# Heads grouped by parity: eight 64x32 TensorE tiles in place of block-diagonal pairs, in a landmark-attention and MLP kernel

## The chip, the cores and the metric

The kernel runs on one core of a Trainium2 chip. The metric is device time in microseconds of one execution. A kernel is timed in several executions; one execution is also recorded by the hardware profiler, and the rows below come from that one.

## The reference, cut to what matters

Eight batches of landmark attention (8 heads, 576 positions, head size 64, 32 landmarks) feed two MLPs. All operands are fp32.

```python
q_lm = q.reshape(B, H, 32, 18, D).mean(axis=3)      # k_lm in the same way
A, Bm, C = sm(q, k_lm), sm(q_lm, k_lm), sm(q_lm, k) # sm: scaled softmax scores
Z = Bm.T / (norm1(Bm) * norminf(Bm) + 1e-6)
for _ in range(6):
    Z = 2 * Z - Z @ Bm @ Z
attn = A @ Z @ C @ v
h = x @ w_in;  g = where(h > 0, h, exp(min(h, 0)) - 1);  x = g @ w_out   # 512 -> 2048 -> 512
y = max(x @ w1, x @ w2, x @ w3) @ w_out2                                  # 512 -> 768 -> 512
```

## The kernel before, in words

q and k arrive transposed, so that 128 partitions hold two heads (64 rows each); `load_qk` brings four heads at a time (`g` is 0 or 1). The attention output is never formed: A, the softmax of q against the landmarks, is multiplied by W' = (Z C v) w_in, which `w_step` makes for each batch out of `m_step`'s 64 values per head and landmark. Phase 1 runs over eight batches `b`, each in 32 slots: a slot is one `h_mm` (six matmuls of A's high and low parts with W', line 597) and one `x_mm` (twelve matmuls with w_out, line 628), so 18 mainline matmuls of 288 columns a slot, 576 a batch. Behind `h_mm` come two ACT operations (relu and exp), a DVE operation, an ACT cast and a POOL or DVE subtraction; `x_mm` follows three slots later (`LAG`). Phase 2 (lines 903 and 1012, the second MLP) follows; the change does not touch it.

The attention of batch b+1 is spread over the slots of batch b: `plan` names the slot behind which each step is emitted (`att_steps` for b of 2 and more, `SECOND_SLOTS` for b of 1). For batch 0 it stands ahead of everything, in the order of the string `ORDER` (B, A and V are three streams of steps, c a step of the weights' conversion). DVE's order there is the program's (`manual_schedule`); elsewhere a list scheduler orders each engine's queue by dependencies and priority, and each engine works its queue in order.

A score matmul takes K = 128: for two heads at once, `sums` has POOL spread the landmark sums into a block-diagonal copy (`qbd`, `kbd`), so that a 128x64 weight tile holds both heads. Two such matmuls, `p2` of 0 and 1, write the lower and the upper 64 partitions of one PSUM bank. Each fp32 matmul stands in the trace as two matmuls and two weight loads. `score_c` (C and Bm, line 278) makes two such pairs for each `g`, one for each half of 288 positions; `score_a` (line 327) does the same for A; `w_step` (line 564) makes one pair of 512 columns for each of four column blocks `n` and each `g`, with the copy `mbd` that `m_step` makes out of a masked copy `v2`. `cv` (line 395) multiplies C with v in five chunks, each a pair of 128 columns of which half is masked away afterwards.

PSUM's eight banks: four for `x_mm` (`ps_x`), two for `h_mm` (`ps_h`), two for the attention and W' (`ps_a`, one bank a tile, two tiles). In batch 0 ahead of the mainline, `att_ps` also hands out the banks of `ps_x`. W' is read out of PSUM by an ACT cast (line 572, the high part) and a DVE subtraction (line 576, the low part).

Of the kernel before, what the change touches and what calls it, by code (L numbers as in the profile page):

```python
# [19 lines left out]
def landmark_attention_mlp_maxout_kernel(  # L20
# [18 lines left out]
    P = 128  # L39
# [24 lines left out]
    SECOND_SLOTS = [4, 5, 6, 6, 7, 7, 8, 11, 11, 11, 12, 12, 12, 13, 13, 13]  # L64
    SECOND_SLOTS += [13, 14, 15, 16, 18, 19, 20, 20, 21, 23, 24, 26, 26, 26, 26]

    ORDER = "BBBBBABVVBAVVBVcBABcVABcABcABccBcBABcAcB"
# [26 lines left out]
    ps_a = tc.alloc_tile_pool(name="ps_a", bufs=2, space=PSUM)  # L94
# [43 lines left out]
    class Conversions:  # L138
# [54 lines left out]

    hm = const.tile([P, 4], F32, name="hm")
    dm = const.tile([P, 2], F32, name="dm")
    pm = const.tile([P, 2], F32, name="pm")
# [7 lines left out]
        out=dm, in_=ident.rearrange("p (h j) -> p h j", h=2), op=ALU.add, axis=AX.X  # L204
    )
    nc.vector.tensor_reduce(
        out=eye, in_=ident.rearrange("p (h j) -> p j h", h=4), op=ALU.add, axis=AX.X
    )
    nc.vector.tensor_tensor(out=pm, in0=hm[:, 0:2], in1=hm[:, 2:4], op=ALU.add)
# [10 lines left out]
    def att_ps(b, name):  # L220

        if b == 0 and spare[0] >= 0:
            spare[0] += 1
            n = spare[0] % 6
            if n < 4:
                return ps_x.tile([P, 512], F32, tag=f"x{n}", name=name)
        return ps_a.tile([P, 512], F32, tag="a", name=name)

    def load_qk(b, g, nm):
        n = S + M if nm == "k" else S  # L230
        t = att.tile([P, 2, n], F32, tag=nm + "T", name=nm + "T", bufs=2)
        src = (k if nm == "k" else q)[b, g * 2 * P : (g + 1) * 2 * P, :]
        nc.sync.dma_start(out=t[:, :, :S], in_=src.rearrange("(r p) s -> p r s", p=P))
        state[nm, b, g] = t
# [10 lines left out]
    def sums(b, g, nm):  # L245
        t = state[nm, b, g]
        if nm == "k":
            so = t[:, :, S : S + M]
        else:
            so = att.tile([P, 2, M], F32, tag="qs", name="qs")  # L250
# [7 lines left out]
        sh = [P, 2, 2, M]  # L258
        nc.gpsimd.tensor_tensor(
            out=bd,  # L260
            in0=so.unsqueeze(2).to_broadcast(sh),
            in1=dm.unsqueeze(1).unsqueeze(3).to_broadcast(sh),
            op=ALU.mult,
        )
        state[nm + "bd", b, g] = bd

    def score_c(b, g):
        kT, qbd = state["k", b, g], state["qbd", b, g]
        if g == 0:
            state["bb", b] = att.tile([P, 4, M], F32, tag="bb", name="bb")  # L270
        e = att.tile([P, S], F32, tag="s", name="e", bufs=2)
        mx = att.tile([P, 2], F32, tag="mx", name="mx")
        pcs = []
        for half in range(2):
            n = HF + (M if half else 0)
            pc = att_ps(b, "pc")
            for p2 in range(2):
                nc.tensor.matmul(  # L278
                    pc[64 * p2 : 64 * p2 + 64, :n],
                    qbd[:, p2].rearrange("p a m -> p (a m)"),  # L280
                    kT[:, p2, half * HF : half * HF + n],
                    start=True,
                    stop=True,
                )
            nc.vector.tensor_reduce(
                out=mx[:, half : half + 1], in_=pc[:, :HF], op=ALU.max, axis=AX.X
            )
            pcs.append(pc)
        nb = att.tile([P, 1], F32, tag="nb", name="nb")
        nc.vector.tensor_scalar(  # L290
            out=nb, in0=mx[:, 0:1], scalar1=mx[:, 1:2], scalar2=-s1, op0=ALU.max, op1=ALU.mult
        )
        nc.vector.tensor_copy(state["bb", b][:, g], pcs[1][:, HF : HF + M])
        sm = att.tile([P, 2], F32, tag="sm", name="sm", bufs=2)
        for half in range(2):
            nc.scalar.activation(
                e[:, half * HF : (half + 1) * HF],
                pcs[half][:, :HF],
                AF.Exp,
                bias=nb,  # L300
                scale=s1,
                accum_out=sm[:, half : half + 1],
            )
        state["e", b, g], state["sm", b, g] = e, sm

    def score_c2(b, g):
        sm = state.pop(("sm", b, g))
        rs = att.tile([P, 3], F32, tag="rs", name="rs", bufs=2)
        nc.vector.tensor_scalar(
            out=rs[:, 2:3],  # L310
            in0=sm[:, 0:1],
            scalar1=sm[:, 1:2],
            scalar2=1e-9,
            op0=ALU.add,
            op1=ALU.add,
        )
        nc.vector.reciprocal(rs[:, 2:3], rs[:, 2:3])
        nc.vector.tensor_scalar_mul(rs[:, 0:2], pm, rs[:, 2:3])
        state["rs", b, g] = rs

    def score_a(b, g):
        qT, kbd = state["q", b, g], state["kbd", b, g]
        x = att.tile([P, 2 * NB2, M], F32, tag="s", name="x", bufs=2)
        for half in range(2):
            pa = att_ps(b, "pa")
            for p2 in range(2):
                nc.tensor.matmul(  # L327
                    pa[64 * p2 : 64 * p2 + 64, :HF],
                    kbd[:, p2].rearrange("p a m -> p (a m)"),
                    qT[:, p2, half * HF : (half + 1) * HF],  # L330
                    start=True,
                    stop=True,
                )
            nc.vector.transpose(
                out=x[:, half * NB2 : (half + 1) * NB2].rearrange("p a m -> p (a m)"),
                in_=pa[:, :HF],
            )
        state["x", b, g] = x
# [19 lines left out]
    def soft_a3(b, g):  # L358
# [6 lines left out]
        af = att.tile([P, S], F32, tag="s", name="af", bufs=2)  # L365
# [11 lines left out]
    def exp_t(b, g):  # L377
        e = state.pop(("e", b, g))
        et = att.tile([P, CH, P], F32, tag="et", name="et")
        pt = att_ps(b, "pe")  # L380
# [3 lines left out]
        p2 = att_ps(b, "pe")  # L384
# [4 lines left out]
    def cv(b, g):  # L389
        et, vn, rs = state.pop(("et", b, g)), state["v", b], state["rs", b, g]  # L390
        pt = att_ps(b, "ptv")
        for c in range(CH):
            n = P if c < CH - 1 else TAIL
            for p2 in range(2):
# [7 lines left out]
        vv = rrs[0][:, g, M : M + D]  # L402
        nc.vector.tensor_scalar_mul(vv, pt[:, :D], rs[:, 0:1])
        nc.vector.scalar_tensor_tensor(
            out=vv, in0=pt[:, D:P], scalar=rs[:, 1:2], in1=vv, op0=ALU.mult, op1=ALU.add
        )
# [77 lines left out]
    def bbt(b):  # L484
        bb, td, rc = state["bb", b], state.pop(("td", b)), state["rc", b]
        for gs in groups(b):
            pt = att_ps(b, "pbb")
# [20 lines left out]
    def newton(b, i):  # L508
        cur, nxt, rd = rrs[i % 2], rrs[(i + 1) % 2], state.pop(("rd", b))
        pvs = []  # L510
        for gs in groups(b):
            pt = att_ps(b, "pn")
# [21 lines left out]
        if i == 5:  # L534
            v2 = att.tile([P, 2, 2, D], F32, tag="rd", name="v2", bufs=2)
            nc.gpsimd.tensor_tensor(
                out=v2,
# [827 lines left out]
```

## Time and profile before

| | |
|---|---|
| median of 3 runs | 1436.78 us (1432.18 to 1437.85) |
| the profiled execution | 1435.57 us, of which 1433.8 us are the span from its first to its last instruction |
| busy share of the span | PE 96%, PEld (weight loads) 88%, DVE 64%, POOL 50%, ACT 48% |
| mean granted TensorE clock | 0.977 of full speed |
| chain that ended last | PE 77%, DVE 10%, DMA 6%, issue 3% |

PE is the matmul engine, PEld its weight loads (they overlap the matmuls), DVE VectorE, ACT ScalarE, POOL GpSimd. A matmul's recorded duration contains its way through the array; the rate is read from starts.

### The profile page before, as it was taken

What the parts mean: (1) busy time and instruction counts of PE and PEld (TensorE: products, weight loads), DVE (VectorE), ACT (ScalarE), POOL (GpSimd) and SP (SyncE); (2) the same over time, 40 slices, a digit from 0 to 9 for tenths busy, and PEclk for the clock granted to TensorE, in tenths of its full rate; (3) what the DMA queues carried; (4) which work ended last, traced back from release to release, by engine and by line L of the source; (5) the groups of instructions that cost most, each with busy time, mean ns of one, the idle gap of its engine ahead of it and who ended that gap; (6) DMA issues with size and microseconds to landing.
All of it is one profiled execution on the core that took longest, in us unless ns stands there. A gap on an engine that the chain in (4) does not pass through costs nothing.

```text
span 1433.8 us, 26970 instructions
## 1 busy us (share of the span) xinstructions
PE 1375.8 (96%) x10312; PEld 1256.5 (88%) x10312; DVE 924.4 (64%) x1687; ACT 683.1 (48%) x1554; POOL 717.7 (50%) x717
## 2 busy tenths in 40 slices
PE   5689999999999999999999899899999999998998
PEld 3378788799798797897897899899999999998998
DVE  7998655556456456556454746867776677687773
ACT  4666555555555555555555574322222223335552
POOL 3776324334334344243243565756666666674543
PEclk6789999999999999999999999999999999999999
DMA  9523214024123122141121212212221222238982
GB/s 360 198 85 125 83 63 143 21 71 146 34 74 115 34 97 92 34 138 50 41 83 45 76 33 82 100 68 84 106 82 53 107 82 88 94 129 288 301 261 80
DMA packets 91586, 152.22 MB, mean 106 GB/s; under 512 B 5312, under 2 KB 49472, under 8 KB 91456
## 3 DMA queue, kind: packets, MB, share of 16 engines
q1 hardware_dynamic: 91456, 150.49, 30.7%
q8 instruction: 81, 1.33, 0.4%
q14 instruction: 49, 0.40, 0.1%
HBM read 99.35 MB, written 51.12 MB: 105 GB/s over the span
## 4 chain that ended last, share of the span: by engine, by line
PE 77%; DVE 10%; DMA 6%; issue 3%; ACT 2%; POOL 2%; SPq 0%; DVEq 0%; ACTq 0%; POOLq 0%
PE p L903 24%; PE x L628 23%; PE ph L597 12%; PE p L1012 9%; PE pw L564 4%; DMA words<-in_moe_w_dram 3%; DVE wf L127 2%; PE ptv L395 1%; DMA words<-in_moe_w_out_dram 1%; PE pa L327 1%; DVE wf L123 1%; PE pc L278 1%; PE pn L515 1%; ACT wf L115 1%; DMA hf<-hs 1%
## 5 line engine op out<-in xcount | busy, mean ns | idle before, releaser
L628 PE MATMUL x<-gt,wo 128*128 128x288 f32 x3072 | 480.0, 302 | 6.3 <-DVE wo L100 2.9
L628 PEld LDWEIGHTS x<-gt,wo 128*128 128x128 f32 x3072 | 426.8, 189 | 64.7 <-issue 28.0
L903 PE MATMUL p<-xo,w 128*128 128x256 f32 x3402 | 412.6, 284 | 4.3 <-ACT xo L745 1.7
L903 PEld LDWEIGHTS p<-xo,w 128*128 128x128 f32 x3402 | 410.2, 191 | 6.7 <-ACT xo L745 3.3
L100 POOL TENSOR_TENSOR gt<-eh,gt 128x288 fp32r<-128x288 f32 x243 | 206.8, 853 | 342.3 <-ACT gt L98 337.6
L597 PE MATMUL ph<-ah,wp 128*128 128x288 f32 x1024 | 252.5, 300 | 11.7 <-DVE eh L607 9.7
L607 DVE SCALAR_TENSOR_TENSOR eh<-eh,ph 128x288 f32<-128x288 f32 x256 | 114.3, 447 | 159.3 <-ACT eh L602 151.7
L784 POOL TENSOR_TENSOR u<-s,v 128x512 f32<-128x512 f32 x99 | 137.2, 1386 | 138.6 <-DVE v L782 138.6
L597 PEld LDWEIGHTS ph<-ah,wp 128*128 128x128 f32 x1024 | 180.2, 190 | 28.8 <-DVE eh L607 13.1
L601 ACT ACTIVATE eh<-ph 128x288 f32<-128x288 f32 x256 | 104.7, 410 | 173.3 <-PE ph L597 157.2
L98 ACT CAST gt<-eh 128x288 fp32r<-128x288 f32 x256 | 110.0, 430 | 88.3 <-DVE eh L607 85.9
L597 PE MATMUL ph<-al,wp 128*128 128x288 f32 x512 | 151.9, 297 | 0.0
L773 ACT COPY s<-p 128x512 f32<-128x512 f32 x99 | 57.9, 585 | 185.0 <-PE p L903 155.3
L1012 PE MATMUL p<-wo,ho 128*128 128x256 f32 x1134 | 136.8, 283 | 5.4 <-ACT ho L1000 4.0
L1012 PEld LDWEIGHTS p<-wo,ho 128*128 128x128 f32 x1134 | 136.1, 192 | 6.0 <-ACT ho L1000 4.4
L602 ACT ACTIVATE eh<-eh 128x288 f32<-128x288 f32 x256 | 113.7, 445 | 5.5
L797 DVE TENSOR_TENSOR t<-p,u 128x512 f32<-128x512 f32 x81 | 55.7, 687 | 65.6 <-POOL u L784 62.7
L597 PEld LDWEIGHTS ph<-al,wp 128*128 128x128 f32 x512 | 97.0, 190 | 0.0
L1002 DVE TENSOR_TENSOR ho<-hf,ho 128x768 fp32r<-128x768 f32 x54 | 66.1, 1248 | 17.7 <-ACT ho L1000 16.9
L910 DVE TENSOR_TENSOR t<-t 128x1024 f32<-128x1024 f32 x54 | 71.5, 1325 | 8.7 <-POOL t L787 3.2
L135 POOL TENSOR_TENSOR wf<-wf,words 128x512 uint32<-128x512 uint32 x40 | 55.1, 1379 | 39.5 <-ACT wf L115 18.5
L564 PE MATMUL pw<-w_in_sb,mbd 128*64 128x512 f32 x256 | 72.0, 645 | 0.5 <-ACT mbd L556 0.5
(143 smaller groups left out, 1593.8 us busy)
## 6 DMA issues: line engine op xcount, KB each, us to landing
hf<-hs SPq DMA_DIRECT2D x63, 384.0 KB, 5.0
hs<-t SPq DMA_DIRECT2D x27, 512.0 KB, 3.2
xs<-xo SPq DMA_DIRECT2D x36, 288.0 KB, 2.6
hs<-s SPq DMA_DIRECT2D x27, 384.0 KB, 3.5
qT<-in_q_dram SPq DMA_DIRECT2D x16, 576.0 KB, 3.8
kT<-in_k_dram SPq DMA_DIRECT2D x16, 576.0 KB, 4.8
words<-in_moe_w_dram SPq DMA_DIRECT2D x9, 1024.0 KB, 5.3
xf<-xs SPq DMA_DIRECT2D x9, 1024.0 KB, 5.0
```

Of the source, the lines that this page charges most:

```text
L98: nc.scalar.copy(hi, src)
L100: eng.tensor_tensor(out=lo, in0=src, in1=hi.bitcast(F32), op=ALU.subtract)
L564: nc.tensor.matmul(pt[64 * p2 : 64 * p2 + 64, :], mbd[:, kk], w_in_sb[:, kk, n * 512 : (n + 1) * 512], start=True, stop=True,)
L597: nc.tensor.matmul(ph[:, :HF], a, c, start=(g == 0 and j == 0), stop=(g == 1 and j == 2))
L601: nc.scalar.activation(e, ph[:, :HF], AF.Relu, scale=-1.0)
L602: nc.scalar.activation(e, e, AF.Exp, scale=-1.0)
L607: nc.vector.scalar_tensor_tensor(out=e, in0=e, scalar=1.0, in1=ph[:, :HF], op0=ALU.subtract, op1=ALU.max)
L628: nc.tensor.matmul(xacc[ec][:, :HF], a, gt[:, c], start=(first and j == 0), stop=(last and j == 2),)
L784: nc.gpsimd.tensor_tensor(out=u57, in0=s57, in1=v.unsqueeze(1).to_broadcast([P, 2, 256]), op=ALU.add)
L903: nc.tensor.matmul(dst, l, r, start=(c == 0 and j == 0), stop=(c == 1 and j == 2))
L910: nc.vector.tensor_tensor(out=t, in0=t, in1=cur, op=ALU.max)
L1012: nc.tensor.matmul(dst, l, r, start=(c == 0 and n == 0), stop=(c == NP - 1 and n == 2))
```

## The change

Heads are grouped by parity: group `g` is now the heads on partitions 64g to 64g+63 of the four two-head tiles `j`. A new function `heads` issues eight matmuls in a row, each with K = 64 and 32 weight columns: tile (g, j) reads partitions 64g.. and writes partitions 32j.. of bank g. So both groups' scores of one half, or both groups' W' of one block `n`, come from one call, on the sums themselves: `qbd`, `kbd`, `mbd`, `v2` and the masks `dm` and `pm` go. `ps_a` becomes one tile of two banks (`bufs=1`), handed out as a pair to every step, also to one that uses a single bank. For b of 1 and more, `score_c` copies the scores out of PSUM with ACT and takes the exp from SBUF. `cv` uses four column tiles of 32 with 64 columns in place of two of 64 with 128. The steps' slots and `ORDER` are written anew.

```diff
-    ORDER = "BBBBBABVVBAVVBVcBABcVABcABcABccBcBABcAcB"
+    ORDER = "BBBBBVVABVVBAVcBABcVABcABcABccBcBABccB"
-    ps_a = tc.alloc_tile_pool(name="ps_a", bufs=2, space=PSUM)
+    ps_a = tc.alloc_tile_pool(name="ps_a", bufs=1, space=PSUM)
...
+            n = spare[0] % 3
+            if n < 2:
+                return [
+                    ps_x.tile([P, 512], F32, tag=f"x{2 * n + g}", name=name) for g in range(2)
+                ]
+        t = ps_a.tile([P, 2, 512], F32, tag="a", name=name)
+        return [t[:, g] for g in range(2)]
...
-        bd = att.tile([P, 2, 2, M], F32, tag=nm + "bd", name=nm + "bd")
...
+    def heads(outs, left, right):
+        with tc.manual_schedule(engines={mybir.EngineType.PE}), tc.high_priority(offset=400):
+            for j in (3, 2, 1, 0):
+                for g in range(2):
+                    nc.tensor.matmul(
+                        outs[g][32 * j : 32 * j + 32],
+                        left(j)[64 * g : 64 * g + 64],
+                        right(j)[64 * g : 64 * g + 64],
+                        start=True,
+                        stop=True,
+                    )
+
+    def score_c(b):
+        direct = b == 0
+        es = [att.tile([P, S], F32, tag="s", name="e", bufs=3) for _ in range(2)]
...
+            pcs = att_ps(b, "pc")
+            heads(
+                [pc[:, :n] for pc in pcs],
+                lambda j: state["qs", b, j // 2][:, j % 2],
+                lambda j: state["k", b, j // 2][:, j % 2, half * HF : half * HF + n],
+            )
+            for g in range(2):
+                nc.vector.tensor_reduce(
+                    out=mx[:, g, half : half + 1], in_=pcs[g][:, :HF], op=ALU.max, axis=AX.X
                 )
...
+                if not direct:
+                    nc.scalar.copy(es[g][:, half * HF : (half + 1) * HF], pcs[g][:, :HF])
...
+    def score_a(b):
+            pas = att_ps(b, "pa")
+            heads(
+                [pa[:, :HF] for pa in pas],
+                lambda j: state["ks", b, j // 2][:, j % 2],
+                lambda j: state["q", b, j // 2][:, j % 2, half * HF : (half + 1) * HF],
+            )
+            for g in range(2):
+                nc.vector.transpose(
...
-            for p2 in range(2):
+            for j in range(4):
                 nc.tensor.matmul(
-                    pt[64 * p2 : 64 * p2 + 64, :P],
-                    et[:n, c, 64 * p2 : 64 * p2 + 64],
-                    vn[:n, c, (2 * g + p2) * P : (2 * g + p2 + 1) * P],
+                    pt[32 * j : 32 * j + 32, :D],
+                    et[:n, c, 32 * j : 32 * j + 32],
+                    vn[:n, c, (2 * j + g) * D : (2 * j + g + 1) * D],
...
+    def w_step(b, n, later=False):
+        mt = state["mt", b]
+        pts = att_ps(b, "pw")
+        heads(
+            pts, lambda j: mt[:, j], lambda j: w_in_sb[:, j, n * 512 : (n + 1) * 512]
+        )
...
+    STEP_SLOTS = dict(
+        q0=0, k0=1, q1=2, k1=3, c=5, c20=6, c21=6, e0=6, cv0=7, e1=8, b=8, b2=9, cv1=10, nb=10,
+        bbt=11, n0=12, n1=13, n2=14, n3=15, n4=16, n5=17, a=18, m=19, a10=19, a20=20, a30=20,
+        a11=21, a21=22, a31=23,
+    )
...
+            at(t0 + NSL + 2 * n - 6, w_step, b, n)
```

## Rows read from the trace of the kernel before

**Rows 1.** Windows: length, busy us (count) of PE, PEld, DVE, ACT, POOL; PEclk; DMA
```profile
0.00:53.00 53.00, 29.72 (x124) 16.55 (x125) 43.91 (x110) 24.79 (x57) 24.18 (x27) 0.65 0.91 328
53.00:141.00 88.00, 74.25 (x484) 61.36 (x484) 81.06 (x147) 62.20 (x145) 61.53 (x51) 0.92 0.36 115
141.00:185.00 44.00, 44.00 (x290) 34.49 (x290) 28.24 (x54) 23.70 (x58) 16.20 (x22) 1.00 0.21 70
386.40:487.30 100.90, 100.46 (x724) 87.28 (x723) 55.62 (x128) 55.96 (x139) 37.67 (x46) 1.00 0.24 79
789.00:1433.00 644.00, 626.33 (x5100) 622.15 (x5098) 443.39 (x628) 237.62 (x466) 390.31 (x345) 0.99 0.34 118
```

**Rows 2.** Timeline of PE, two W' pairs: start, us, operation, count
```profile
464.07 0.29 PE L597 MATMUL ph<-ah,wp 128*128 128x288 f32 x1
...
464.86 0.83 PE L628 MATMUL x<-gt,wo 128*128 128x288 f32 x5
465.62 1.08 PE L564 MATMUL pw<-w_in_sb,mbd 128*64 128x512 f32 x4
466.63 0.93 PE L628 MATMUL x<-gt,wo 128*128 128x288 f32 x5
...
468.27 1.08 PE L564 MATMUL pw<-w_in_sb,mbd 128*64 128x512 f32 x4
```

**Rows 3.** Timeline of PE around two pairs of score_a
```profile
247.01 0.71 PE L327 MATMUL pa<-qT,kbd 128*64 128x288 f32 x4
247.65 1.20 PE L628 MATMUL x<-gt,wo 128*128 128x288 f32 x7
248.78 0.71 PE L327 MATMUL pa<-qT,kbd 128*64 128x288 f32 x4
```

**Rows 4.** Timeline of PE around one group's score_c (two pairs)
```profile
387.05 1.25 PE L278 MATMUL pc<-kT,qbd 128*64 128x288 f32 x8
388.22 2.25 PE L628 MATMUL x<-gt,wo 128*128 128x288 f32 x15
390.31 0.29 PE L597 MATMUL ph<-ah,wp 128*128 128x288 f32 x1
```

**Rows 5.** Timeline of PE around one group's cv
```profile
409.25 1.46 PE L395 MATMUL ptv<-v,et 128*64 128x128 f32 x20
410.64 1.85 PE L628 MATMUL x<-gt,wo 128*128 128x288 f32 x12
412.33 0.29 PE L597 MATMUL ph<-ah,wp 128*128 128x288 f32 x1
```

**Rows 6.** Line 564 alone, windows: PE and PEld busy (count), PEclk, DMA
```profile
465.60:465.64 0.04, 0.02 (x2) 0.02 (x2) 1.00 0.00 0
...
466.09:466.12 0.03, 0.03 (x4) 0.00 (x0) 1.00 0.00 0
```

**Rows 7.** Groups by line, 386.4 to 487.3: how W' leaves PSUM
```profile
L576 DVE TENSOR_TENSOR wp<-pw,wp 128x512 fp32r<-128x512 f32 x8 | 5.5, 682 | 1.0 <-ACT wp L572 0.3
...
L572 ACT CAST wp<-pw 128x512 fp32r<-128x512 f32 x8 | 4.7, 587 | 0.8 <-PE pw L564 0.2
```

**Rows 8.** What PE waited for from 185 to 789: total, times, longest
```profile
PE pn L515 <- DVE rr L528: 1.9, 5, 0.4
```

**Rows 9.** Timeline: the last pair of a batch's score_a on PE, and DVE's transposes of it
```profile
450.37 0.71 PE L327 MATMUL pa<-qT,kbd 128*64 128x288 f32 x4
...
457.52 0.83 DVE L334 STREAM_TRANSPOSE x<-pa 128x288 f32<-128x288 f32 x2
```

**Rows 10.** Timeline of the stretch ahead of the mainline: first scores, last sum, v2, first W'
```profile
6.74 2.36 PE L278 MATMUL pc<-kT,qbd 128*64 128x288 f32 x8 [6.74 <-POOL qbd L259]
...
9.59 1.35 DVE L251 TENSOR_REDUCE kT<-kT 128x64 f32<-128x1152 f32 x1
...
45.46 0.99 POOL L536 TENSOR_TENSOR v<-rr,pm 128x256 f32<-128x256 f32 x1 [2.61 <-DVE rr L528]
...
48.20 3.68 PE L564 MATMUL pw<-w_in_sb,mbd 128*64 128x512 f32 x8 [0.46 <-ACT mbd L556]
```

More of the change, by code (lines that the diff above doesn't have):

```diff
@@ L256, in sums @@
         )
-        bd = att.tile([P, 2, 2, M], F32, tag=nm + "bd", name=nm + "bd")
[L258 to L273, printed above, removed]
+        state[nm + "s", b, r] = so
@@ new lines, in score_c @@
+        nc.vector.tensor_reduce(out=nb, in_=mx, op=ALU.max, axis=AX.X)
+        nc.vector.tensor_scalar_mul(nb, nb, -s1)
+        for g in range(2):
+            e = es[g]
+            sm = att.tile([P, 2], F32, tag="sm", name="sm", bufs=2)
+            if direct:
+                for half in range(2):
+                    nc.scalar.activation(
+                        e[:, half * HF : (half + 1) * HF],
+                        kept[half][g][:, :HF],
+                        AF.Exp,
+                        bias=nb[:, g : g + 1],
+                        scale=s1,
+                        accum_out=sm[:, half : half + 1],
+                    )
+            else:
+                nc.scalar.activation(
+                    e, e, AF.Exp, bias=nb[:, g : g + 1], scale=s1, accum_out=sm[:, 0:1]
+                )
+            state["e", b, g], state["sm", b, g] = e, sm
@@ L319, in score_c2 @@
+        if b == 0:
+            nc.vector.tensor_scalar(
+                out=rs,
+                in0=sm[:, 0:1],
+                scalar1=sm[:, 1:2],
+                scalar2=1e-9,
+                op0=ALU.add,
+                op1=ALU.add,
+            )
+        else:
+            nc.vector.tensor_scalar_add(rs, sm[:, 0:1], 1e-9)
+        nc.vector.reciprocal(rs, rs)
         state["rs", b, g] = rs
-    def score_a(b, g):
-        qT, kbd = state["q", b, g], state["kbd", b, g]
-        x = att.tile([P, 2 * NB2, M], F32, tag="s", name="x", bufs=2)
+    def score_a(b):
+        xs_ = [
+            att.tile([P, 2 * NB2, M], F32, tag="s", name="x", bufs=3) for _ in range(2)
+        ]
@@ L340, in soft_a1 @@
+        for g in range(2):
+            state["x", b, g] = xs_[g]
     def soft_a1(b, g):
@@ L1054, in att_steps @@
-            (9, lambda: soft_b2(b)),
-            (10, lambda: cv(b, 1)),
-            (10, lambda: norm_b(b)),
-            (11, lambda: bbt(b)),
+            ("q0", lambda: sums(b, 0, "q")),
+            ("k0", lambda: sums(b, 0, "k")),
+            ("q1", lambda: sums(b, 1, "q")),
+            ("k1", lambda: sums(b, 1, "k")),
+            ("c", lambda: score_c(b)),
+            ("c20", lambda: score_c2(b, 0)),
+            ("c21", lambda: score_c2(b, 1)),
+            ("e0", lambda: exp_t(b, 0)),
@@ L1143, in w_both @@
         conv.upto(index["in", n * KD + KD - 1] + 1)
-        return [w_step(0, n, g, True) for g in range(2)]
+        return w_step(0, n, True)
     def w_end(n):
@@ L1184, in landmark_attention_mlp_maxout_kernel @@
     conv.upto(KD)
[L1185 to L1186 removed]
+    for fn in w_step(0, 0, True):
         gate = fn()
```

229 lines of the change are left out of this document (76 added, 153 removed).

## Prediction

> **What bounds the kernel now.** I read the windows by stage first [rows 1]. In a middle batch of phase 1, 100.9 us long, PE is busy for 100.46 us, at a granted clock of 1.00 (the 2.4 GHz level), while DVE, ACT and POOL are busy for 56, 56 and 38. The table of PE's waits [rows 8] names 1.9 us in five waits, its longest entry, from 185 to 789 us. So what PE issues is the length of a batch there, and a microsecond that it is spared is a microsecond of the kernel. From 141 to 185 PE is busy for the whole 44.00 us as well. From 53 to 141 it is not the bound: DVE is busy for 81 of 88 us, PE for 74. Ahead of 53 us the clock is 0.65 on average and PE idles for nearly half the time: there the end is set by a chain through DVE. Phase 2, 789 to the end, is as full of PE work, none of which the change touches.
>
> Then I priced PE's pieces in the timeline, by starts. A mainline matmul takes one step of 0.132 us: six `h_mm` steps lead from 464.07 to 464.86 [rows 2]. Between the starts of two W' pairs lie 2.65 us and eleven such steps (1.45), so that a W' pair with its way in and out costs 1.20 us. Two pairs of `score_a` lie 1.77 us apart with seven steps (0.92) between them [rows 3]: 0.85 each. For `score_c` [rows 4] 15 steps follow, 3.26 - 1.98 = 1.28; the way in, which this difference does not hold, is 0.10 in rows 2 (464.86 and five steps give 465.52, the pair starts at 465.62). So 1.38 for one group, two pairs back to back. `cv` in the same way [rows 5]: 3.08 - 1.58 + 0.10 = 1.60.
>
> What the reader is to see next is that tiles already run side by side. In [rows 6] both `p2` tiles of a W' pair have their first matmul under way within the first 40 ns; the second two join within 30 ns at 466.09, so that the pair is two waves of two, 0.48 us apart, and not four matmuls in a row.
>
> **The change part by part.** *Scores and W'.* Today a batch spends 2 x 1.38 = 2.76 us on C, 4 x 0.85 = 3.40 on A and 8 x 1.20 = 9.60 on W': 15.76 us. Afterwards it is two, two and four calls of eight tiles. If eight tiles share the two waves as two do now, a call costs today's pair and the starts of six more tiles, for which I take 0.01 us each (two start within the 40 ns window): 0.85 + 0.05 = 0.90 for scores, 1.20 + 0.05 = 1.25 for W'. That is 1.8 + 1.8 + 5.0 = 8.6, a gain of 7.2 us a batch. Whether tiles in the upper and the lower 64 partitions run together is what no row shows; that they don't is a rival below. The other bound, tiles that are no cheaper in fours than in twos, is that rival's upper end. The Trainium skill, TensorE: Matmul & The Clock Gate, Part 3 ("Measured speedup vs the span model"), has row and column tiles running together, 16 of them, with about 4 ns a tile; by it a call would cost 0.03 us less than I take, and the sum would be 1390 us. No run so far shows it for this shape.
>
> This gain counts in full for the attention of batches 2 to 7, which runs beside six PE-bound batches: 6 x 7.2 = 43.2 us. Of batch 1, `score_a` (1.6) and W' (4.6) fall into the PE-bound stretch from 141 to 185: 6.2 us. Its `score_c` and batch 0's W' fall between 53 and 141, where DVE sets the time: nothing, at most 0.96 for the scores and 3 x 1.15 for the blocks, 4.4 us, if PE counted there. Sum: 49.4 us.
>
> *cv.* Ten pairs in waves become ten fours with half the columns. A call's 1.60 us less the way in and out (0.10 each) is 0.14 a wave, an estimate. If a wave shrinks with its columns, half of that goes: 0.7 a call, 1.4 a batch. If a wave is bound by its number of instructions, which doubles, a call gets 1.4 dearer, a batch 2.8. The nearest row is its own, ten waves in either case; I take 0, with -8 and +17 us over six batches as ends.
>
> *The one place in PSUM.* Every step now takes both banks and waits until the step before has left them. For the newton steps, `bbt`, `cv` behind `exp_t`, and `m_step` this adds nothing, since each already needs the result that the evacuation makes. W' calls come every second slot, some six us apart; the release takes the call, one cast and two subtractions in turn, 1.25 + 0.59 + 2 x 0.68 = 3.2 us [rows 7], so PE finds the place free. New waits are three a batch: the second half of `score_c` and of `score_a` behind the first half's evacuation, `exp_t` of group 1 behind `cv` of group 0. Behind such a waiting matmul stand mainline `h_mm` and `x_mm` in PE's queue, and ACT's relu waits for those. The scheduler can put mainline work between the halves, as it does now between dependent newton steps; where it is a little wrong PE waits like the newton steps do [rows 8], up to 0.4 each. I take 0.25 a place, 0.75 a batch, 5 us over seven batches; ends 0 and 1.5 us a place (two transposes of 0.42 [rows 9] and the matmuls' own way out).
>
> The Trainium skill, TensorEngine Tiling (Array Packing), "PSUM Bottleneck", speaks against the change: tiling quickens TensorE and leaves the emptying of PSUM as slow as it was. By it a W' call would cost its two subtractions, 1.36 us, not 1.25, and the sum would be about 1395 us. The row speaks against that here: DVE is free for 45 of 100.9 us [rows 1].
>
> *Other engines.* POOL loses the four masks and `v2` of a batch, DVE two small operations a group; neither sets a batch's time. ACT gets four copies of 288 columns and has two long exps for four short ones: at most 4 x 0.59 (the row of a 512-column cast [rows 7]) on 56 us, covered by 45 idle. If that cover were gone, it would delay relu and so `x_mm` three slots later. No DMA is added or passed; SP's queue sees its transfers sooner, at a DMA share of 0.24.
>
> *Ahead of the mainline* [rows 10]. C's scores start at 6.74 today with one group; now they need all four sums, so not before 10.94, and their exps come some 2 us later, with DVE waiting. On the other side the masked copy `v2` (0.99) leaves the chain into `m_step`, and W' of block 0, 3.68 us at the low clock, halves. I take 0, with 3 us either way.
>
> *Sum.* 49.4 - 5.3 = 44 us off. The profiled execution took 1435.57 us (its span is 1433.8, and 1.8 lie around it); the median is 1436.78, 1.2 above. 1435.6 - 44 gives **1392 us**. With the ends of the small terms (cv, places, start, the stretch from 53 to 141) not all taken together, the forecast's own range is 1377 to 1406.
>
> **The rivals.**
>
> *Row tiles take turns.* The two groups' tiles share columns of the array, and every wave becomes two. A score call then costs up to 0.85 + 2 x 0.29 = 1.4 us (the wave of 288 columns estimated at 0.29 from 0.48 for 512), a W' call 1.20 + 0.96 = 2.2. A batch: 2.8 + 2.8 + 8.8 = 14.4 for 15.76 today, 1.4 us gained; with six batches, 1 us of batch 1 and the 5 us of waits it ends at 1431. If the second load of weights hides, some 0.05 a wave comes back and it is 1425. For it: no row of before has two row tiles. Against: the column tiles run freely.
>
> *The place stalls PE in part.* The three new waits cost their end of 1.5 us each: 4.5 x 7 = 31 us, and 49 - 31 leaves 1418. For it: PE's queue is in order, and two slots of slack are no help within one step. Against: newton steps wait little.
>
> *Slower: `score_a` holds the place.* DVE took the last transposes of a batch 6.5 us after their matmuls had left (451.0 to 457.5 [rows 9]), because its queue had other work first. Today the two banks just stay full. With one place, the second half's call and then `m_step` stand behind such a release in PE's queue. If PE has no other work queued ahead of them, each costs up to 6.5 us; the gain of 7 us a batch is gone at 7 us of such waits a batch, and both together, 13 us in seven batches, give 1435.6 - 49 + 91 = 1478. Against: the scheduler knows of the release and moves these calls behind mainline work.
>
> **How the numbers follow.** Chances: the forecast 0.67, row tiles in turns 0.13, place in part 0.13, slower 0.07. Differences under 0.5% (7 us) can hardly be told from none here. Faster by more: the forecast, the second rival and half of the first, 0.86; the same: the other half of the first, 0.07; slower 0.07. The range of 1375 to 1425 holds the forecast with its own range, the second rival and part of the first, about 8 in 10.
>
> **What would show it.** In the profile after: a middle batch of about 94 us in place of 100.9, with PE still busy throughout; the calls of eight with all eight first matmuls starting within 0.1 us, score calls at 0.90 us and W' calls at 1.25 by the same differences of starts; PE's waits for DVE or ACT under a microsecond a batch. Two starts a wave within a call, or the second group's 0.3 us or more behind the first's, would speak for row tiles in turns. Waits of PE ahead of the second halves, named with the reductions of `mx`, the copies of `e` or the transposes of `x`, would speak for the place. The prediction is wrong if a batch shortens by less than 4 us, if DVE or ACT becomes what PE waits for in the mainline, or if the first W' call, which starts at 48.20 us now [rows 10], moves by more than 3 us.

## The result, and the profile after

The changed kernel took 1450.51 us, the median of four runs, beside 1436.37 for the kernel before in the same comparison: a ratio of 1.010, 95% interval 1.0068 to 1.0132. It is 1% slower. I had predicted 1392 us, 3% faster, and 0.07 for slower.

The profiled execution took 1451.51 us with a span of 1449.5. The windows of the kernel after (length, busy us and count of PE, PEld, DVE, ACT, POOL; PEclk; DMA share, GB/s) answer to [rows 1]: the stretch ahead of the first expert step (the first `h_mm`), batch 0, one middle batch from its first `h_mm` to the next batch's, and that batch cut in two.

```profile
0.00:63.40 63.40, 22.12 (x202) 11.94 (x202) 41.61 (x104) 28.05 (x63) 23.95 (x25) 0.72 0.79 286
63.43:190.10 126.67, 104.04 (x834) 88.56 (x834) 101.84 (x183) 77.85 (x180) 66.92 (x58) 0.90 0.30 98
285.80:389.20 103.40, 97.46 (x843) 85.77 (x843) 54.26 (x124) 56.30 (x140) 35.19 (x41) 0.95 0.22 77
...
285.80:296.00 10.20, 7.27 (x52) 3.40 (x60) 7.34 (x15) 4.71 (x11) 3.13 (x4) 0.58 0.17 59
296.00:389.20 93.20, 90.19 (x799) 82.36 (x795) 46.92 (x110) 51.59 (x130) 32.05 (x37) 0.99 0.23 79
```

The first `h_mm` begins at 63.4 us instead of 52.7. Batch 0 takes 126.7 us instead of 120.4. Batches 1 to 6 together take 602.5 instead of 606.8, and what follows 656.8 instead of 653.8 (2.8 of these 3.0 in batch 7, up to its last `x_mm`). So the loss of 15.7 us in the span is 10.7 at the start, 6.3 in batch 0 and 3.0 at the end, and the steady batches, where I had put nearly the whole gain, return 4.3.

Inside the middle batch the ten microseconds at its front are the odd ones: PE is busy for 7.27 of 10.20 us and the granted clock averages 0.58, close to the 1.2 GHz level; PE had stood idle for 2.4 us ahead of the first `h_mm` and idled again behind it. In the remaining 93.2 us the clock is 0.99. Before, a middle batch ran at 1.00 throughout [rows 1]. What PE waited for from 185 to 789 us (total, times, longest) answers to [rows 8]:

```profile
PE pw L262 <- DVE wp L573: 15.0, 12, 2.3
PE ph L598 <- ACT ah L96: 9.6, 5, 2.4
PE pn L524 <- DVE rr L537: 1.5, 2, 0.8
```

The Newton steps wait as before. New are W' waiting for its place to be emptied, and `h_mm` at a batch's front waiting for `ah`: the attention of the next batch is not ready at the boundary. The timeline of PE's attention work in that batch (start, us, line, operation, count; a matmul of this type has two records, so a call of eight shows x16) tells why:

```profile
301.89 0.72 PE L262 MATMUL pc<-kT,qs 64*32 64x288 f32 x16
307.66 0.77 PE L262 MATMUL pc<-kT,qs 64*32 64x320 f32 x16
314.16 0.60 PE L394 MATMUL pe<-ident,e 128*128 128x128 f32 x4
317.91 0.27 PE L396 MATMUL pe<-ident,e 128*64 128x128 f32 x1
321.44 0.90 PE L406 MATMUL ptv<-v,et 128*32 128x64 f32 x40
325.29 0.60 PE L394 MATMUL pe<-ident,e 128*128 128x128 f32 x4
...
336.62 0.60 PE L497 MATMUL pbb<-bb,td 128*128 128x128 f32 x4
...
366.25 0.61 PE L524 MATMUL pn<-rr,rd 128*128 128x128 f32 x4
369.82 0.72 PE L262 MATMUL pa<-qT,kT 64*32 64x288 f32 x16
374.28 0.71 PE L262 MATMUL pa<-qT,kT 64*32 64x288 f32 x16
...
378.73 0.44 PE L548 MATMUL pm<-bbd,rr 128*64 128x128 f32 x4
382.36 1.09 PE L262 MATMUL pw<-w_in_sb,mt 64*32 64x512 f32 x16
388.12 1.09 PE L262 MATMUL pw<-w_in_sb,mt 64*32 64x512 f32 x16 [2.06 <-DVE wp L573]
392.03 1.96 PE L262 MATMUL pw<-w_in_sb,mt 64*32 64x512 f32 x16 [0.64 <-DVE wp L573]
397.69 1.96 PE L262 MATMUL pw<-w_in_sb,mt 64*32 64x512 f32 x16
403.96 0.71 PE L262 MATMUL pc<-kT,qs 64*32 64x288 f32 x16
```

Twenty uses of the one place stand one behind the other. None is long, but from a use to the next there is its evacuation and then the mainline work that stands ahead of the next use in PE's in-order queue: 102.07 us from one batch's first score call to the next batch's, 5.1 us a use. That is as long as the batch. W' runs past the boundary at 389.20, partly at the low clock (1.96 us for a call in place of 1.09), and DVE has the four sums of the next batch in its queue there (1.35 us each at 378.93, 380.52, 383.02 and 384.46), so that W' 0's low parts leave only at 386.69.

To see what PE's time goes to, I added up, over batches 2 to 6, the distances between the starts of all PE records. A distance between two mainline matmuls counts as mainline; any other counts as the insertion's (the attention matmuls that stand between two of the mainline), less one step of 0.133 us on the way in. The first step behind an insertion is longer, 0.23 us on average in the kernel before, and counts as mainline: a W' pair stands here at 1.10 where the prediction, with its way out, has 1.20. Left out are the transposes, `bbt` and `m_step`, 1.6 to 1.8 us a batch (2.6 in the last row). In us a batch, with the experiments below:

```
kernel                      batch  mainline  score_c  cv    Newton  score_a  W'
before                      100.8  79.1      2.53     3.04  2.94    2.81     8.79
after                       101.4  81.4      1.53     1.84  2.58    1.47    10.94
e1_two_places                99.2  79.5      2.20     2.16  2.92    2.75     8.04
n4_after (4 Newton steps)    93.1  79.5      1.53     1.84  1.82    1.47     5.31
n4_before (4 Newton steps)  101.7  79.6      2.53     3.04  2.28    2.57     9.92
f2_whole_two_places          93.2  79.0      1.52     2.16  2.79    1.47     4.57
n4_f2 (4 Newton steps)       93.8  79.3      1.53     2.47  1.91    1.47     5.54
e2_before_one_place         122.1  81.5      3.01     2.96  4.37   12.28    15.36
```

From before to after, scores and `cv` cost 3.5 us less; W', whose matmuls were halved, costs 2.2 more, since PE's waits and the low clock fall into it; and the mainline costs 2.4 more. Of these 2.1 lie in the stretches in which the granted clock is at its lower level: 12.8 mainline steps a batch take 3.8 us there, where at 0.133 us each they would take 1.7.

### The profile page after: what moved, and what is told of

The parts are those of the page before. It is cut to its first block, busy times and chain, and to the rows that moved or that the text cites. A ratio compares the mean times of both kernels' runs of the same rounds, so it can differ in the third digit from the quotient of the medians.

```text
span 1449.5 us, 28545 instructions
## 1 busy us (share of the span) xinstructions
PE 1335.1 (92%) x11144; PEld 1243.0 (86%) x11144; DVE 911.6 (63%) x1653; ACT 686.9 (47%) x1554; POOL 698.3 (48%) x677
## 4 chain that ended last, share of the span: by engine, by line
PE 70%; DVE 12%; DMA 7%; ACT 4%; issue 4%; POOL 2%; SPq 0%; DVEq 0%; POOLq 0%; ACTq 0%
PE p L904 24%; PE x L629 20%; PE ph L598 12%; PE p L1013 8%; DMA words<-in_moe_w_dram 3%; PE pw L262 2%; DMA words<-in_moe_w_in_dram 1%; DVE wp L573 1%; DMA qT<-in_q_dram 1%; PE pn L524 1%; DVE tt L713 1%; DMA hf<-hs 1%; DVE wf L125 1%; PE ptv L406 1%; ACT wp L568 1%
## 5 line engine op out<-in xcount | busy, mean ns | idle before, releaser
L629 PE MATMUL x<-gt,wo 128*128 128x288 f32 x3072 | 469.9, 300 | 2.9 <-DVE gt L98 1.5
L98 POOL TENSOR_TENSOR gt<-eh,gt 128x288 fp32r<-128x288 f32 x243 | 203.4, 840 | 353.6 <-ACT gt L96 323.9
L598 PE MATMUL ph<-ah,wp 128*128 128x288 f32 x1024 | 265.6, 315 | 27.4 <-DVE eh L608 11.9
L598 PEld LDWEIGHTS ph<-ah,wp 128*128 128x128 f32 x1024 | 187.2, 198 | 68.8 <-DVE eh L608 29.3
L598 PE MATMUL ph<-al,wp 128*128 128x288 f32 x512 | 158.7, 310 | 1.6 <-POOL al L98 1.4
L598 PEld LDWEIGHTS ph<-al,wp 128*128 128x128 f32 x512 | 102.0, 199 | 7.6 <-POOL al L98 5.3
L133 POOL TENSOR_TENSOR wf<-wf,words 128x512 uint32<-128x512 uint32 x40 | 54.8, 1372 | 58.6 <-DVE wf L125 52.7
L1001 ACT CAST ho<-hf 128x768 fp32r<-128x768 f32 x63 | 51.4, 836 | 41.6 <-PE p L1013 23.7
```

Of the source, the lines that this page charges most:

```text
L98: eng.tensor_tensor(out=lo, in0=src, in1=hi.bitcast(F32), op=ALU.subtract)
L598: nc.tensor.matmul(ph[:, :HF], a, c, start=(g == 0 and j == 0), stop=(g == 1 and j == 2))
L629: nc.tensor.matmul(xacc[ec][:, :HF], a, gt[:, c], start=(first and j == 0), stop=(last and j == 2),)
```

## The experiments

Theory: the one place, with its twenty uses in a row, sets the batch. Rivals: the tiles themselves or the order of the calls in PE's queue are at fault; for the start, ScalarE's order or the conversions.

**1. Two places again.**

```diff
-    ps_a = tc.alloc_tile_pool(name="ps_a", bufs=1, space=PSUM)
+    ps_a = tc.alloc_tile_pool(name="ps_a", bufs=2, space=PSUM)
-        t = ps_a.tile([P, 2, 512], F32, tag="a", name=name)
-        return [t[:, g] for g in range(2)]
+        return [ps_a.tile([P, 512], F32, tag="a", name=name) for _ in range(banks)]
```

(`cv`, `bbt`, Newton and `m_step` ask for one bank.)

> The changed kernel with its two PSUM banks handed out singly again: a call of eight tiles takes two, and the steps that need one bank (the line-406 products, bbt, Newton, m) take one. Everything else of the change stays. Theory 'one place': in the changed kernel some twenty uses of the place follow one another in each batch, about 5.1 us each, and fill it (102 us); with two places the next use can start while the last is being evacuated, so W' ends inside its batch, the dips of the granted clock at the batch boundaries go, and each of batches 1 to 7 falls from 98.6 us on average to some 94 to 96, near what the prediction had from the saved matmuls. 1410 to 1430 us; the first expert step still comes near 63 us, not 53. Rival 'the tiles or their order in PE's queue are at fault' (eight-tile calls, the priority of the heads helper): the place is not what waits, 1445 to 1455 us, dips and late W' stay.

Measured: 1441.44 us, ratio 1.0023 (1.0002 to 1.0044). The waits on the place and the dips of the clock went, as the theory has it; PE is busy for 98.41 of 98.60 us. The time did not follow: 99.2 us a batch, not 94 to 96, and batch 0 takes 131.4 us, 4.7 more than in the changed kernel. Its window and its timeline around W':

```profile
290.70:389.30 98.60, 98.41 (x829) 85.41 (x828) 53.79 (x122) 55.85 (x140) 35.45 (x41) 1.00 0.24 81
```

```profile
370.52 1.09 PE L261 MATMUL pw<-w_in_sb,mt 64*32 64x512 f32 x16
376.68 1.04 PE L261 MATMUL pw<-w_in_sb,mt 64*32 64x512 f32 x2
379.04 1.08 PE L261 MATMUL pw<-w_in_sb,mt 64*32 64x512 f32 x14
```

One of the eight matmuls goes alone as soon as its bank is free, the other seven follow 2.4 us later when the second bank is. The one alone takes 1.04 us, the seven 1.08, all eight together 1.09: a call in two pieces costs twice. By the table the pieces cost some 5 us a batch.

**2. A shorter chain.** Four Newton steps instead of six, in the changed kernel and, as a control, in the kernel before. Two of six updates of the inverse are left out.

```diff
-        if i < 5:
+        if i < 3:
-        for i in range(6):
+        for i in range(4):
```

> The changed kernel with four Newton steps instead of six (two of the six updates of the inverse are left out). Theory 'one place': two uses fewer in the chain that sets a batch, about 5 us each, so batches 1 to 7 shorten by 4 to 10 us each, until TensorE's own work (some 94 us) sets them; with 5 to 8 us at the start, 1385 to 1415 us. Rival 'TensorE's work sets the batch': two Newton steps are 4 matmuls, about 0.9 us of TensorE a batch; 7 us in all and 5 to 8 at the start: 1435 to 1440 us.

> The kernel before with the same two Newton steps left out: the control to the run before. Theory 'one place': with two banks handed out singly the chain is not what sets a batch, so only TensorE's 0.9 us a batch and the start's two steps (5 us) are gained: 1420 to 1432 us, a gain of 5 to 16. If a chain of steps set the batch of this kernel as well, it would gain as much as the changed kernel does, 35 to 65 us, and the place would not be what differs.

Measured: 1396.26 us (ratio 0.9697, 0.9659 to 0.9736) and 1441.84 us (1.0028, 1.0004 to 1.0051). In the changed kernel two steps, 0.8 us of PE's time a batch by the table, take 8.3 us off a batch, as the theory had it. In the kernel before they take off nothing; there the first expert step came 3.9 us sooner, and the later batches gave it back (101.7 us, W' 9.92 instead of 8.79), so my 5 to 16 us were a miss. The chain sets a batch with one place and not with two.

**3. The kernel before with one place.** Tiles, heads and copies as before.

```diff
-    ps_a = tc.alloc_tile_pool(name="ps_a", bufs=2, space=PSUM)
+    ps_a = tc.alloc_tile_pool(name="ps_a", bufs=1, space=PSUM)
-        return ps_a.tile([P, 512], F32, tag="a", name=name)
+        return ps_a.tile([P, 2, 512], F32, tag="a", name=name)[:, 0]
```

(`score_c` uses both banks for its two halves.)

> The kernel before with one place of two banks in place of two of one bank: every use takes the place, and uses one of its banks (score_c's pair uses both). Heads, tiles and copies are those of before. Theory 'one place': some 26 uses a batch at 4 to 5 us each are 105 to 130 us against 100.7: 1470 to 1650 us, with W' past the batch boundary and the granted clock at 1.2 GHz there. Rival 'the tiles or their order are at fault': they are not in this kernel, so 1436 to 1445 us.

Measured: 1588.58 us, one run, inside the theory's range. Batches of 122 us at a clock of 0.89, and waits of PE from 185 to 789 us that [rows 8] has not got:

```profile
PE pa L329 <- DVE x L336: 31.1, 8, 9.2
PE pw L566 <- DVE wp L578: 9.4, 10, 2.0
```

The place alone, without the new tiles, makes the loss, and more of it. Of the 21 us a batch that it costs, 9.5 stand at `score_a`, which waits for transposes in DVE's queue, and 6.6 at W'.

**4. Whole calls by a section of the scheduler.** Two places, and the eight matmuls of `heads` as one section; with and without the exponentials of batch 0 moved ahead (experiment 5); and one place with the section as a control.

```diff
-        with tc.manual_schedule(engines={mybir.EngineType.PE}), tc.high_priority(offset=400):
+        with tc.high_priority(offset=400), tc.tile_critical():
```

> Two one-bank places as in e1_two_places, and the eight matmuls of a call kept together in TensorE's queue (heads makes them one section for the scheduler). In e1_two_places the waits on the place were gone and TensorE was 99.7% busy at a clock of 1.00, but a batch took 99.2 us, since many calls stood in two pieces: one matmul alone in one gap of the mainline and seven in the next. Insertions a batch there: score_c 2.20 us in 3.0 pieces against 1.53 in 2 in the run with four Newton steps, score_a 2.75 against 1.47, W' 8.04 in 7.4 pieces against 5.31, line 406 2.16 against 1.84: 5.0 us. Theory 'pieces': without them a batch takes 94 to 95 us, what the prediction had, and the whole 1441 - 7 x 4.6 = 1409 us, 1400 to 1416. Rival 'the whole call waits in its turn': a call that needs both banks at once waits for the later one at the head of TensorE's queue, and the batch stays at 98 to 101 us: 1435 to 1450.

> As e1c_whole_calls, and in batch 0 the four exponentials of line 302 stand ahead of the first widening in ScalarE's queue. In the changed kernel they waited for it: the maxima were there at 14.07 us, the widening waited for its words until 15.17, the first exponential began at 17.56. Theory 'start by ScalarE's order': the chain that leads to the first expert step moves up by up to 3.4 us, so 1 to 3.5 us less than e1c_whole_calls. Rival 'the conversions set the start': the widening comes 2 us later, the narrowing on VectorE waits for it, and the first expert step is no earlier: 0 to +3 us.

> The control to e1c_whole_calls: the changed kernel with its one place of two banks, and the same section around the eight matmuls of a call (its calls were whole already). The section also changes where the scheduler puts the calls. Theory 'one place': the uses still follow one another and about fill a batch, W' ends at the boundary or past it: 98 to 101 us a batch, 1435 to 1452 us. Rival 'the order in the queue, not the place': with the calls put earlier the saved matmuls show with one place too: 94 to 96 us a batch, 1405 to 1420 us.

Measured: 1518.36 us (1.0595, 1.0555 to 1.0634), 1519.92 (1.0599, 1.057 to 1.0628) and 1550.80 (1.0815, 1.0785 to 1.0846). The first and the third missed with theory and rival alike. Of the second, beside the first, the rival's 0 to 3 us came out: 1.6 us more, the first expert step at 76.9 us beside 76.7. The section is at fault: alone, without the second place, it makes the changed kernel 100 us slower. PE's waits of the first show calls that wait for work they don't need, as for the mainline's `eh`, for `gt` and for a load of the next batch's keys.

```profile
PE pw L261 <- DVE eh L607: 12.8, 4, 3.5
PE pw L261 <- DMA kT<-in_k_dram: 3.0, 1, 3.0
PE pc L261 <- POOL gt L98: 2.8, 4, 1.4
```

Of the pieces this says nothing. It does say that with the same section two places are 32 us better than one.

**5. The start, by ScalarE's order.** The changed kernel, with the first widening queued behind batch 0's exponentials. (The weights are converted in two steps: a *widening*, two ScalarE operations, lines 113 and 114, and a *narrowing*, two VectorE operations, lines 121 and 125, and a sum on POOL.)

```diff
+            with tc.issue_after(state["exp"].ins):
+                next(conv.run, None)
```

> The changed kernel with that reordering of ScalarE's start alone, one place as it is. Read from the first expert step (63.4 us in the changed kernel, 52.7 before). Theory 'start by ScalarE's order': 60 to 62 us. Rival 'the conversions set the start': 63 us or later. The batches stay as in the changed kernel, so 1445 to 1453 us in all.

Measured: first expert step at 62.4 us, 1454.90 us in all (one run). That is one microsecond of the 10.7, and it lies between the two: 0.4 us above the theory's range, 0.6 below the rival's. The whole, 1454.90 us, is 2 us above the range. The wait for the exponentials fell from 4.6 to 2.5 us, and the wait for the first narrowing rose from 1.3 to 2.5.

**6. Whole calls by fixed places.** A call's group 0 always takes place 0 and group 1 place 1; single-bank steps take a named place; the last two matmuls of a call change sides, so that place 1, for which the first matmul waits, is the last to come free.

```diff
-                for g in range(2):
+                for g in (1, 0) if j else (0, 1):
-        t = ps_a.tile([P, 2, 512], F32, tag="a", name=name)
-        return [t[:, g] for g in range(2)]
+        both = range(2) if bank is None else [bank]
+        return [ps_a.tile([P, 512], F32, tag=f"a{i}", name=name) for i in both]
-        pt = att_ps(b, "ptv")[0]
+        pt = att_ps(b, "ptv", 1 - g)[0]
-        banks = att_ps(b, "pn")
+        banks = att_ps(b, "pn", i % 2 if b else None)
```

> The changed kernel with two places of one bank, each with a fixed name: group 0 of a call always takes place 0 and group 1 place 1, the steps that need one bank take a named one, and the last two of a call's eight matmuls change sides, so that place 1, for which a call's first matmul waits, is also the last to come free. In TensorE's queue all eight stand together then, without the section that made e1c_whole_calls wait for other engines. Theory 'pieces' (e1_two_places lost 5.0 us a batch to calls in two pieces, and one place costs the changed kernel its late W'): insertions fall from 19.7 us a batch in e1_two_places to some 14.5 to 15, a batch takes 94 to 95 us with the clock at 1.00, and the whole 1405 to 1415 us. Rival 'the whole call waits in its turn': no batch below 98 us, 1435 to 1450.

Measured: 1397.49 us, ratio 0.971 (0.9693 to 0.9728): 2.9% faster than the kernel before, and below the 1405 to 1415 us that the theory gave. A batch takes 93.2 us. Its window of a middle batch, PE's wait for W' to be emptied from 185 to 789 us, and the timeline that answers to the chain above:

```profile
367.50:460.50 93.00, 92.60 (x829) 84.45 (x828) 53.52 (x123) 55.55 (x141) 35.85 (x42) 1.00 0.26 86
```

```profile
PE pw L262 <- DVE wp L573: 0.5, 2, 0.2
```

```profile
374.82 0.72 PE L262 MATMUL pc<-kT,qs 64*32 64x288 f32 x16
379.91 0.77 PE L262 MATMUL pc<-kT,qs 64*32 64x320 f32 x16
385.67 0.60 PE L394 MATMUL pe<-ident,e 128*128 128x128 f32 x4
386.11 0.27 PE L396 MATMUL pe<-ident,e 128*64 128x128 f32 x1
389.65 0.90 PE L406 MATMUL ptv<-v,et 128*32 128x64 f32 x40
392.05 0.60 PE L394 MATMUL pe<-ident,e 128*128 128x128 f32 x4
...
401.21 0.61 PE L497 MATMUL pbb<-bb,td 128*128 128x128 f32 x4
...
429.07 0.61 PE L524 MATMUL pn<-rr,rd 128*128 128x128 f32 x4
...
444.52 1.09 PE L262 MATMUL pw<-w_in_sb,mt 64*32 64x512 f32 x16
...
462.40 1.09 PE L262 MATMUL pw<-w_in_sb,mt 64*32 64x512 f32 x16
467.76 0.72 PE L262 MATMUL pc<-kT,qs 64*32 64x288 f32 x16
```

From the first score call to `bbt` it is 26.4 us instead of 34.7: the fifth transpose of group 0 follows the first four after 0.44 us (386.11) instead of 3.75 (317.91), and group 1's transposes follow `cv` of group 0 after 2.4 us instead of 3.9. From `bbt` to the last Newton step the two are alike (27.9 and 29.6), because there each step needs the result of the step before. The last W' call starts at 462.40, two microseconds past the boundary of 460.50, and at the full clock.

**7. The control to experiment 2.** The same with four Newton steps.

> f2_whole_two_places with four Newton steps instead of six: the control to n4_after. Theory 'one place': with two places the chain of uses no longer sets the batch (f2 has 93.16 us a batch at a clock of 1.00, TensorE's own work), so leaving out two steps gives only their matmuls back, 0.9 us of 2.79, and 5 to 8 us at the start: 92.2 to 92.6 us a batch, 1383 to 1392 us in all. Rival 'a chain of steps still sets the batch': some 4 us a batch or more, 1350 to 1365 us.

Measured: 1394.27 us (0.9719, 0.9685 to 0.9753), 93.8 us a batch; first expert step 52.9 us instead of 59.2. Nothing a batch instead of 8.3: the chain has let go. That a batch is 0.7 longer and not 0.7 shorter was not expected; PE's waits from 185 to 789 us include 3.1 us for W' low parts and 6.3 for `eh`, against 0.5 and 3.8 in experiment 6; the order of the queue came out a little less good.

**8. The start, by VectorE's order.** Fixed places, batch 0's scores copied out, exponentials ahead of the widening, and `score_a` and `soft_b` ahead of what needs exponentials; then the first narrowings moved ahead of line 413 too.

```diff
-    ORDER = "BBBBBVVABVVBAVcBABcVABcABcABccBcBABccB"
+    ORDER = "BBBBBABVVVVBAVcBABcVABcABcABccBcBABccB"
```

```diff
-    ORDER = "BBBBBABVVVVBAVcBABcVABcABcABccBcBABccB"
+    ORDER = "BBBBBABVVcVVBAVBABcVABcABcABccBcBABccB"
```

> f2_whole_two_places with another start. VectorE's order is fixed there and it is busy nearly throughout, so the theory 'VectorE's idle time sets the start' counts its idle stretches ahead of the first expert step: 6.7 us before, 17.6 in the changed kernel, 10.9 more, and the first step comes 10.7 us later. Of these 4.6 are the wait for the exponentials, 2.5 for transposes, 4.8 for the first W' at the end. Here batch 0's scores are copied out as in the later batches (ScalarE has nothing to do then), the exponentials stand ahead of the first widening, and VectorE's order has score_a and soft_b ahead of what needs the exponentials. Expected by that theory: 4 to 7 us of idle time less, the first step at 56 to 60 us instead of some 62, 1400 to 1410 us in all. Rival 'the conversions set the start': VectorE waits for the widening instead and the first step stays at 61 us or later.

> s2_start_early with VectorE's first two narrowings moved ahead of line 413, for which it waited 4.1 us there (17.6 to 21.7 us); elsewhere the same. Theory 'VectorE's idle time sets the start': idle time ahead of the first expert step falls from 12.5 us to 9 to 11, the first step comes at 56 to 58.5 us instead of 59.4, and the whole at 1394 to 1398. Rival 'ScalarE's widenings set the start': the line-413 product stays late because its copy stands behind four widenings in ScalarE's queue, VectorE waits for the widening or for line 413 all the same, and the first step stays at 59 to 61 us.

Measured: 1399.99 us (0.974, 0.972 to 0.976) and 1397.30 (0.9726, 0.9701 to 0.9752); first expert step at 59.4 and 56.0 us, against 59.2 in experiment 6. The first lies in its theory's range of 56 to 60, but that was written against some 62 us, and experiment 6 has 59.2: nothing moved. VectorE stopped waiting for the exponentials and waited for line 413 instead, whose operand, the copy of line 395, stood behind four widenings (two operations each) in ScalarE's queue. Two rows of its timeline:

```profile
19.55 0.58 ACT L395 COPY et<-pe 128x512 f32<-128x512 f32 x1
...
21.70 0.28 DVE L413 TENSOR_SCALAR rr<-ptv,rs 128x64 f32<-128x64 f32 x1 [4.12 <-PE ptv L406]
```

The second moved the first expert step by 3.4 us, as its theory said, but batch 0 took 129.2 us instead of 123.5, and the whole stayed the same.

## Why the prediction was wrong

Between the 44 us off that I forecast and the 15.7 on that the span shows lie 60. By the prediction's own terms some 34 of them belong to batches 1 to 6 (38.7 off, of which 4.3 came), 11 to the start, 12 to batch 0 and 3 to the end.

**The price of a call: right.** Tiles in the upper and the lower 64 partitions do run together. In the windows of line 262 in the changed kernel eight matmul records, one of each tile, are under way within 0.1 us of the start of a W' call (382.36), and the whole call is 1.09 us long where a pair was 1.08 [rows 2]:

```profile
382.40:382.46 0.06, 0.06 (x8) 0.06 (x16) 1.00 0.60 230
```

Counted as in the table, 18 of the 20 W' calls of experiment 6 in batches 2 to 6 cost 1.11 us where each of the 40 pairs before cost 1.10; the other two hold a wait, which makes the mean 1.14 (4.57 / 4). A `score_a` call costs 0.73, and so did a pair of it that stood alone. I had taken 0.05 more than a pair; it is 0.01. *Row tiles take turns* falls. The Trainium skill, TensorE: Matmul & The Clock Gate, Part 3, has about 4 ns for a further tile, which makes, as an estimate, 0.02 us for six. The 0.01 measured here is nearer to that than to my 0.05.

**cv: the size was off.** I took 0 with ends of -1.4 and +2.8 us a batch. It gained 1.2 (3.04 to 1.84), near the end at which a wave shrinks with its columns.

**"The one place in PSUM": the step that failed.** I asked of each step whether it *must* wait for the one before, found three new waits a batch, and took 0.25 us each. I never added the uses up. For the steps that depend on each other the place indeed adds nothing, and the Newton steps bear that out (27.9 and 29.6 us). But the sum is 20 uses at 5.1 us, 102 us in a batch that was to take 94. The 5.1 is more than the call and its evacuation, which I had at 3.2 us for W' [rows 7]; it holds the way back through PE's queue too. The sentence "PE finds the place free" took W' calls to stand six us apart with slack behind them; at the end of a full chain there is none, and 15.0 us of PE's waits fall on them. With the place undone, and calls kept whole, the same tiles give 93.2 us a batch: 7.7 less than before, where I had 7.2 for scores and W' and 6.4 after the charge for the waits. By the table's columns 6.6 of the 7.7 are scores and W', and 0.9 is `cv`, which I had at 0. So a term that I put at 0.75 us a batch was about 8 (101.4 - 93.2). That experiment 6 as a whole comes near my 1392 us is in part luck: its batches 1 to 6 give 49.1 us, ten more than I had summed, and its start and batch 0 take 9.5 back. The Trainium skill, TensorEngine Tiling (Array Packing), "PSUM Bottleneck", has the emptying of PSUM stay as slow as it was. I set it against DVE's free time. The trace agrees with the page's mechanism, 15.0 us of PE's waits on W' being emptied, where two places leave 0.5 (experiment 6). How W' is emptied around the boundary:

```profile
386.69 1.28 DVE L573 TENSOR_TENSOR wp<-pw,wp 128x512 fp32r<-128x512 f32 x2
...
389.36 1.06 ACT L568 CAST wp<-pw 128x512 fp32r<-128x512 f32 x2
...
390.60 1.28 DVE L573 TENSOR_TENSOR wp<-pw,wp 128x512 fp32r<-128x512 f32 x2
```

At the first call (382.36) it is DVE's order that makes PE wait: the sums and the softmax of A stand ahead of the low parts, which start 2.1 us after their casts have ended (383.56 and 1.07). At the second (388.12) casts and subtractions follow the call with hardly a gap, and the third call still waits 0.64 us. Neither is seen in a share of busy time.

**What came with it.** I left out the clock. PE, kept at 100.46 of 100.9 us before [rows 1], idled at every boundary from 285.8 us on, and the granted clock fell to the lower level there; the mainline cost 2.4 us a batch more, 2.1 of them at the lower level. In experiments 1 and 6 both were gone: no stretch of a batch from 2 to 6 is at the lower level there.

**"Ahead of the mainline", 0 with 3 either way: failed too.** The first expert step came 10.7 us later, and the first W' call, which I had allowed 3 us, 10.3 (58.48 instead of 48.20). Rows of the changed kernel's start:

```profile
10.03 2.62 PE L262 MATMUL pc<-kT,qs 64*32 64x288 f32 x32 [10.03 <-DMA kT<-in_k_dram]
...
15.17 0.66 ACT L113 ACTIVATE w_in_sb<-words 128x512 f32<-128x512 f32 x1 [13.15 <-DMA words<-in_moe_w_in_dram]
...
17.56 0.48 ACT L302 ACTIVATE e<-pc,nb 128x288 f32<-128x288 f32 x1
...
18.65 0.21 DVE L320 TENSOR_SCALAR rs<-sm 128x1 f32<-128x1 f32 x1 [4.58 <-ACT e L302]
...
58.48 1.96 PE L262 MATMUL pw<-w_in_sb,mt 64*32 64x512 f32 x16 [0.45 <-ACT mt L556]
...
62.80 1.07 ACT L568 CAST wp<-pw 128x512 fp32r<-128x512 f32 x2
...
63.90 1.29 DVE L573 TENSOR_TENSOR wp<-pw,wp 128x512 fp32r<-128x512 f32 x2 [4.80 <-ACT wp L568]
```

I had seen the later scores (10.03 instead of 6.74) and set W's halving against them (1.96 us it is, for 3.68 [rows 10]). I had not seen that the exponentials then fall behind the first widening in ScalarE's queue, and that VectorE, whose order is fixed, then has no work. Its busy time ahead of the first expert step hardly differs (43.62 us before, 41.61 after); its idle time does, 21.8 us (63.40 - 41.61) against 9.1 (52.70 - 43.62). (The expectation in experiment 8 counts only the longer stretches, 17.6 and 6.7.) Of the 10.7 us, 1.8 went with the place in experiment 1 and 4.2 in experiment 6; 3.2 more went with VectorE's order (experiment 8) and came back in batch 0. No single wait is the cause: two of three reorderings only moved the wait on. What the rest of the start and batch 0's 6.3 us consist of stays open; after experiment 6, 6.5 and 3.0 us of them are left. In batch 0 the longest wait of PE is the one ahead of batch 1's first score call, 6.0 us in the changed kernel, for which the profile names no engine; in experiment 6 it is 4.0 us, for W' low parts, and before it was 1.5.

**The rivals.** *The place stalls PE in part* had the right resource and about half its size (4.5 us a batch), at other steps than those I named. *Slower: `score_a` holds the place* had the right sign and the right mechanism, a release behind other work in DVE's queue; in the changed kernel it struck W' and not `score_a`, whose transposes there start 0.85 us after the call (374.28 and 375.13 us), and in experiment 3 it struck just where I had put it (31.1 us in eight waits). I gave the two 0.20 together because I priced them as accidents of a few waits.

## What to carry to other kernels

When a change makes a buffer single, list every use of it in one round, multiply by the distance from a use to the next as the trace has it (the work, the evacuation and the way back through the in-order queue), and compare the sum with the round that you hope for, not with the present one. Matmuls that are to share the array are worth their price only if they stand together in the queue: see to it that the operand or bank that comes last is the one the first of them waits for. For a prologue whose order is fixed on one engine, list that engine's idle stretches before and after, and not what the change takes off another: here its busy time hardly moved, and its idle time grew by 12.7 us.

## What the runs showed of the hardware

A 64x32 tile's matmul of 512 columns alone took 1.04 us, eight of them together 1.09 (experiment 1): the eight were all but free, and one left behind cost a whole call. With fewer Newton steps the kernel before got no faster although its first expert step came 3.9 us sooner; PE was busy for 100.82 of 101.10 us in a middle batch. The split of experiment 1 is found there too: in batches 2 to 6 three W' matmuls stood together eight times (1.95 us) and one by itself eight times (1.09), where two pairs cost 2.20. That is 1.3 us a batch, more than the 0.7 that the Newton steps gave.
